# The shared port of two engines as a lock in a list scheduler, fewer identity products, and a new order of the head

## The chip, the cores and the metric

One NeuronCore of a Trainium2 chip runs the whole program in one launch. The metric is the device time of that launch in microseconds. TensorE (PE, with its weight loads PEld), VectorE (DVE), ScalarE (ACT), GpSimd (POOL) and the DMA queue of SyncE (SP) each run their own instructions in order and wait for each other by semaphores.

## What is computed

Packed attention, then two expert layers, all in float32. Cut to what matters:

```python
p_packed = sm_attn(p, k, v)              # 4 batches x 8 heads, 32 packed rows, 576 keys, head size 64
x = sm_attn(q, p_packed, p_packed)       # 2304 tokens x 512
h = x @ w_in                             # first MoE: 512 -> 2048
x = (h * np.cos(h)) @ w_out              # 2048 -> 512
p = domain_probs / (domain_probs.sum(-1, keepdims=True) + 1e-09)
for e in range(4):                       # second MoE: 512 -> 1024 -> 512, four experts
    out += p[:, e:e + 1] * (np.maximum(x @ w1[e], 0.0) @ w2[e])
```

`w_in` and `w_out` of the first MoE arrive as float64 and are turned into float32 on the chip, word by word.

## The kernel before

**Products.** Each large float32 product is three TensorE products of a rounded high part and a low part (`mm3`). A "split" makes them: ScalarE writes the high part, GpSimd subtracts it from the value for the low part.

**Work of the first MoE.** The attention comes in eight units n (two for each batch bb). `attn_p` of a unit has the scores (`f_s1`, TensorE), their maximum and its negative (`f_mx`, VectorE), `f_exp` (ScalarE), a transpose (`f_tr`) and its copy (`f_aT`), the product with v (`f_pv`), `f_z`, a transpose `f_pp` and a copy `f_ptf`. `attn_q` has the scores of q (`f_s2`), then on VectorE, GpSimd and ScalarE a softmax over groups of 32 (`f_x`, `f_m2`, `f_sub`, `f_exp`, `f_z2`, `f_mul`, `f_xt`) and the split `f_hi`, `f_lo` into tile `at`. The expert layer runs over 16 pairs (G, bb), G a group of 512 hidden columns: `m_front` (8 products, tile `m`), four `a_front` (12 products each, then round, remainder, abs, sin, multiply, and a split into `g`), and four `a_back` (24 products each, then an evacuation into `yacc`). PSUM has four slots (`pa`): an `a_front` holds its slot until its multiply (`f_mul`, DVE) is done.

**Weights.** `w_block` turns a block of 256 x 512 words into float32: an absolute value (`f_and`), a clamp (`f_clamp`), a shift (`f_shift`), the sign (`f_sign`, two inputs), a scaling of the low words (`f_low`), an add (`f_add`, GpSimd), and for w_out a split. In the blocks of G 0 and 1 (`head`) `f_and` is on ScalarE and `f_clamp` on GpSimd; later both are on VectorE.

**The order.** Class `Plan` lists these operations with an engine, a cost in us, what they follow, the buffers they take, and a key. `Plan.run` is a list scheduler: over and over it takes, of the operations that are ready, the one that can start first (the smaller key on a tie). The planned start times then give the order in which every engine's instructions are written; waits on the chip come from the data. Keys stand in a table `KEYS`: for the pairs of units at the start (`a0`, `a2`), for the first expert pairs (`m00`, `f00`, `m01`), and for each later pair 100 n plus `m`, `f` (four `a_front`), `b` (four `a_back`), `att`, `blk`.

**Identity products.** Where the plan leaves TensorE idle for over 1 us before 60 us, products of a 128x128 identity are put in (`idle`); each such group takes a PSUM slot too.

**The second MoE** is written out at hand-made times counted from the end of the plan (`BASE`), 24 steps of 31 us. Its first splits (`t_f` and later) fall among the last `a_front` results of the first MoE.

## Time and profile before

| | us |
|---|---|
| two runs | 1219.58 and 1222.03, median 1220.8 |
| the profiled execution | 1224.17 |
| its span, first to last instruction | 1222.4 |
| TensorE busy in the span | 1163.9 (95%) |
| VectorE, ScalarE, GpSimd busy | 711.1, 537.5, 639.5 |
| mean granted TensorE clock | 0.976 |

The profiled execution lies 3.4 us over the median of the two runs. Matmuls are pipelined: one recorded as 0.29 us can follow the last after 0.13 us. A granted clock of 1.0 is 2.4 GHz, 0.5 is 1.2 GHz. In a row, the bracket at the end gives the idle time of that engine just before and what ended it. The busy share over the whole span hides where TensorE waits: the table by stretches further down separates the first 160 us from what follows.

### The profile page before, as it was taken

To read this page: it belongs to the slowest core of one execution; us is meant where nothing else is said; L and a number is where in the kernel's file an instruction comes from. 1 tells how busy PE (TensorE), PEld (TensorE's weight loads), DVE (VectorE), ACT (ScalarE), POOL (GpSimd) and SP (SyncE) were. 2 spreads that over 40 slices of the span, in tenths; PEclk is the share of its full clock that TensorE was granted. 3 is DMA by queue.
4 is the path that set the end of the run, shared out by engine and by line. 5 is a ranking of instruction groups with operands and counts; after the bars stand their busy time and mean duration, and the time that the engine had idled before them with its cause. 6 is when DMAs were issued, how large, how long until landed. Compare 5 with 4: busy or idle time off the path is not lost.

```text
span 1222.4 us, 17304 instructions
## 1 busy us (share of the span) xinstructions
PE 1163.9 (95%) x6884; PEld 1045.2 (86%) x6884; DVE 711.1 (58%) x1050; ACT 537.5 (44%) x891; POOL 639.5 (52%) x415
## 2 busy tenths in 40 slices
PE   7687899999999988999999999999999999999997
PEld 5476778999989987999999889999998899999996
DVE  3657679684444547555555765555557655555543
ACT  3466676666555544333333433333334333333320
POOL 2767586445223367555555864445556755555520
PEclk9788999999999998999999999999999999999999
DMA  9726243332112532222242132222331332221201
GB/s 276 234 103 224 78 147 143 112 109 78 39 48 98 170 112 87 69 69 70 70 121 69 59 107 77 70 69 69 93 97 52 93 97 69 69 65 62 64 1 52
DMA packets 54162, 115.98 MB, mean 95 GB/s; under 512 B 5824, under 2 KB 18112, under 8 KB 52032
## 3 DMA queue, kind: packets, MB, share of 16 engines
q1 hardware_dynamic: 54080, 114.87, 29.7%
q8 instruction: 54, 0.88, 0.3%
q14 instruction: 28, 0.23, 0.1%
HBM read 100.70 MB, written 14.16 MB: 94 GB/s over the span
## 4 chain that ended last, share of the span: by engine, by line
PE 82%; DVE 5%; ACT 2%; issue 1%; POOL 1%; DMA 1%; SPq 0%; DVEq 0%; POOLq 0%; ACTq 0%
PE pa L185 27%; PE pa L187 27%; PE pa L186 26%; PE pa L489 2%; DVE s L634 1%; DVE g L704 1%; DVE p L691 1%; DVE ys L659 1%; DVE oacc L752 0%; POOL dt L246 0%; DVE t L523 0%; DMA ys<-y 0%; ACT t L530 0%; POOL g L540 0%; DVE yacc L581 0%
## 5 line engine op out<-in xcount | busy, mean ns | idle before, releaser
L185 PE MATMUL pa<-w,g 128*128 128x512 f32 x576 | 227.2, 394 | 6.2 <-DVE oacc L752 6.2
L691 DVE TENSOR_TENSOR p<-pa,p 128x384 f32<-128x384 f32 x240 | 133.6, 557 | 170.6 <-PE pa L187 104.8
L187 PE MATMUL pa<-w,g 128*128 128x512 f32 x576 | 227.3, 395 | 2.7 <-DVE g L704 2.7
L185 PE MATMUL pa<-bop,aop 128*128 128x384 f32 x672 | 226.2, 337 | 3.1 <-DVE g L704 1.6
L186 PE MATMUL pa<-w,g 128*128 128x512 f32 x576 | 226.7, 394 | 0.0
L187 PE MATMUL pa<-bop,aop 128*128 128x384 f32 x672 | 226.2, 337 | 0.1
L186 PE MATMUL pa<-bop,aop 128*128 128x384 f32 x672 | 226.2, 337 | 0.0
L609 POOL TENSOR_TENSOR w<-raw,w 128x512 fp32r<-128x512 f32 x96 | 137.3, 1440 | 148.0 <-ACT w L608 148.0
L540 POOL TENSOR_TENSOR g<-t,g 128x576 fp32r<-128x576 f32 x64 | 95.8, 1499 | 162.4 <-ACT g L537 146.7
L609 POOL TENSOR_TENSOR aop<-s,aop 128x512 fp32r<-128x512 f32 x96 | 135.3, 1418 | 85.2 <-ACT aop L608 82.3
L698 ACT ACTIVATE g<-p 128x384 fp32r<-128x384 f32 x144 | 75.6, 525 | 216.4 <-DVE p L691 213.4
L609 POOL TENSOR_TENSOR aop<-raw,aop 128x512 fp32r<-128x512 f32 x72 | 111.4, 1548 | 94.0 <-ACT aop L608 65.0
L185 PE MATMUL pa<-g,w 128*128 128x288 f32 x512 | 154.6, 302 | 2.0 <-ACT a L340 0.8
L186 PE MATMUL pa<-g,w 128*128 128x288 f32 x512 | 152.0, 297 | 2.9 <-POOL g L540 2.9
L187 PE MATMUL pa<-g,w 128*128 128x288 f32 x512 | 151.2, 295 | 0.0
L752 DVE SCALAR_TENSOR_TENSOR oacc<-pa,pr,oacc 128x512 f32<-128x512 f32 x126 | 94.1, 748 | 85.2 <-PE pa L187 85.2
L185 PEld LDWEIGHTS pa<-bop,aop 128*128 128x128 f32 x672 | 126.7, 189 | 9.5 <-DVE p L691 2.4
L187 PEld LDWEIGHTS pa<-w,g 128*128 128x128 f32 x576 | 109.1, 189 | 27.4 <-DVE g L704 3.5
L185 PEld LDWEIGHTS pa<-w,g 128*128 128x128 f32 x576 | 109.2, 190 | 26.9 <-DVE oacc L752 8.3
L186 PEld LDWEIGHTS pa<-bop,aop 128*128 128x128 f32 x672 | 126.7, 188 | 5.0
L187 PEld LDWEIGHTS pa<-bop,aop 128*128 128x128 f32 x672 | 126.6, 188 | 0.4 <-POOL aop L609 0.4
L186 PEld LDWEIGHTS pa<-w,g 128*128 128x128 f32 x576 | 109.2, 190 | 18.9
(102 smaller groups left out, 1991.4 us busy)
## 6 DMA issues: line engine op xcount, KB each, us to landing
raw<-w SPq DMA_DIRECT2D x96, 512.0 KB, 3.7
at<-at SPq DMA_DIRECT2D x16, 1152.0 KB, 5.2
raw<-w_in SPq DMA_DIRECT2D x8, 1024.0 KB, 6.6
raw<-w_out SPq DMA_DIRECT2D x8, 1024.0 KB, 5.3
kt<-kT SPq DMA_DIRECT2D x8, 576.0 KB, 10.1
vt<-vk SPq DMA_DIRECT2D x8, 576.0 KB, 13.1
qt<-qT SPq DMA_DIRECT2D x8, 576.0 KB, 14.4
y<-yacc SPq DMA_DIRECT2D x24, 192.0 KB, 2.2
```

Of the source, the lines that this page charges most:

```text
L185: nc.tensor.matmul(o, lhsT=l(0), rhs=r(0), start=first, stop=False, skip_group_check=True)
L186: nc.tensor.matmul(o, lhsT=l(0), rhs=r(1), start=False, stop=False, skip_group_check=True)
L187: nc.tensor.matmul(o, lhsT=l(1), rhs=r(0), start=False, stop=last, skip_group_check=True)
L489: nc.tensor.matmul(o[64 * a:64 * a + 64, g], lhsT=ptfs[2 * bb + g][:, 64 * a:64 * a + 64], rhs=w[g]["D"].bitcast(F32)[:, a ^ (bb % 2)], st ...
L540: nc.gpsimd.tensor_tensor(out=s["g"][:, 1], in0=s["t"], in1=s["g"][:, 0].bitcast(F32), op=ALU.subtract)
L609: nc.gpsimd.tensor_tensor(out=dst[:, 1], in0=src, in1=dst[:, 0].bitcast(F32), op=ALU.subtract)
L634: nc.vector.tensor_tensor(out=t, in0=b[x], in1=b[y], op=o)
L659: nc.vector.tensor_tensor(out=t, in0=ysd[x], in1=ysd[y], op=ALU.subtract)
L691: nc.vector.tensor_tensor(out=s[o] if o in s else tmp(o), in0=s[x], in1=s[y], op=ALU.add)
L698: nc.scalar.activation(g[:, 0], s[src], AF.Relu)
L704: nc.vector.scalar_tensor_tensor(out=g[:, 1], in0=s[src], scalar=0.0, in1=g[:, 0].bitcast(F32), op0=ALU.max, op1=ALU.subtract)
L752: nc.vector.scalar_tensor_tensor(out=oaccs[k], in0=o, scalar=sc, in1=oaccs[k], op0=ALU.mult, op1=ALU.add)
```

## The change

Four things:

1. The plan knows a lock: every GpSimd operation, and every VectorE operation marked `port`, may start only when the last such operation has ended. The mark is on the four VectorE steps of `w_block` and the small reductions' second steps; `f_mx` and `f_z2` are cut in two so that only the second part carries it. No wait is written for the lock into the program: it moves only the order. Costs are changed to smaller ones throughout, the latency between engines from 0.07 to 0.1, the rate of transfers from 0.29 to 0.27.
2. `f_clamp` of the head's eight blocks goes from GpSimd to VectorE (ten instructions).
3. Identity products are put only into gaps whose end lies before 31 us of the plan, and fewer for each us of gap: 22 where there were 56, beside the 14 at the very start.
4. Another table of keys.

```diff
-    def op(self, eng, us, f, after=(), take=(), use=(), key=None, table=None):
+    def op(self, eng, us, f, after=(), take=(), use=(), key=None, table=None, port=False):
...
-             "use": list(use) + list(take), "key": key, "table": table, "n": len(self.ops), "next": [],
+             "use": list(use) + list(take), "key": key, "table": table, "port": port or eng == "POOL", "n": len(self.ops), "next": [],
...
-                    t = max(o["at"], free.get(eng, 0.0))
+                    t = max(o["at"], free.get(eng, 0.0), port if o["port"] else 0.0)
...
+            port = t + us if o["port"] else port
...
-                (nc.gpsimd if head else nc.vector).tensor_scalar(out=d, in0=d, scalar1=F64_LO, scalar2=F64_HI, op0=ALU.max, op1=ALU.min)
+                nc.vector.tensor_scalar(out=d, in0=d, scalar1=F64_LO, scalar2=F64_HI, op0=ALU.max, op1=ALU.min)
...
-            a = pl.op(*("POOL", 1.1 * r) if head else ("DVE", 1.2 * r), f_clamp, [a], [], [sd], key)
-            a = pl.op("DVE", 1.2 * r, f_shift, [a], [], [sd], key)
-            a = pl.op("DVE", 1.37 * r, f_sign, [a], [], [sraw, sd], key)
+            a = pl.op("DVE", 0.72 * r, f_clamp, [a], [], [sd], key, port=True)
+            a = pl.op("DVE", 0.72 * r, f_shift, [a], [], [sd], key, port=True)
+            a = pl.op("DVE", 1.1 * r, f_sign, [a], [], [sraw, sd], key, port=True)
...
-            "blk": -81, "blk0": 61, "m": 32.5, "m0": 105, "f": (-3, 24, 40, 71), "f0": (-4, 10, 57, 72.5),
-            "b": (14, 30, 94, 97), "b0": (2, 54, 98, 101)}
+            "blk": -71, "blk0": 59, "m": 1, "m0": 96, "f": (5, 15, 53, 56), "f0": (10, 23, 41, 73),
+            "b": (17, 48, 72, 93), "b0": (-60, 34, 87, 93)}
...
-        if a["end"] < 60 and b["start"] - a["end"] > 1:
-            plan.append((a["end"], len(plan), lambda n=int((b["start"] - a["end"] - 0.5) / 0.25): idle(n)))
+        if b["start"] < 31 and b["start"] - a["end"] > 1:
+            plan.append((a["end"], len(plan), lambda n=int((b["start"] - a["end"] - 0.5) / 0.3): idle(n)))
```

**What moves, place 1.** VectorE while the second block of `w_in` is converted and units 2 and 3 get their maxima (lines before: L250 shift, L255 sign, L333 maximum, L335 its negative, L427 to L429 sum and reciprocal, L436 transpose, L354 and L355 of unit 2). Before:

```order
L250 TENSOR_SCALAR wd<-wd 128x512 x2
L427 TENSOR_REDUCE z_377<-x 128x18
L428 TENSOR_SCALAR z_377<-z_377 128x18
L429 RECIPROCAL z_377<-z_377 128x18
L333 TENSOR_REDUCE mx<-pa 128x1
L335 TENSOR_SCALAR nb<-mx 128x1
L255 SCALAR_TENSOR_TENSOR wd<-raw_263,wd 128x512
L436 STREAM_TRANSPOSE xt<-x 128x576
L255 SCALAR_TENSOR_TENSOR wd<-raw_263,wd 128x512
```

The same block in the changed kernel (L248 clamp, L252 shift, L257 sign, L336 maximum, L341 its negative, L434 sum):

```order
L248 TENSOR_SCALAR wd<-wd 128x512
L336 TENSOR_REDUCE mx<-pa 128x1
L252 TENSOR_SCALAR wd<-wd 128x512
L248 TENSOR_SCALAR wd<-wd 128x512
L257 SCALAR_TENSOR_TENSOR wd<-raw_266,wd 128x512
L252 TENSOR_SCALAR wd<-wd 128x512
L434 TENSOR_REDUCE z_352<-x 128x18
L336 TENSOR_REDUCE mx<-pa 128x1
L257 SCALAR_TENSOR_TENSOR wd<-raw_266,wd 128x512
L341 TENSOR_SCALAR nb<-mx 128x1 x2
```

The two clamps are new in the row, the last sign stands behind the maximum of unit 3, and the transposes and reciprocals come after the whole block.

**Place 2.** TensorE from the end of the first four `a_front` to the first `a_back` (L185 to L187 `mm3`, L404 scores of q, L328 scores of the next units, L826 identity products). Before:

```order
L186 MATMUL pa<-at,m 128x288
L187 MATMUL pa<-at,m 128x288
L826 MATMUL pa<-ident 128x128 x19
L404 MATMUL pa<-qt,ptf 64x288 x8
L328 MATMUL pa<-kt,pbd 64x288 x8
L185 MATMUL pa<-g,w 128x288
```

In the changed kernel (L187 to L189 `mm3`, L378 a transpose of unit 3, L411 scores of q, L500 `m_front` of the second pair):

```order
L188 MATMUL pa<-at,m 128x288
L189 MATMUL pa<-at,m 128x288
L378 MATMUL pa<-ident,pz 128x128
L411 MATMUL pa<-qt,ptf 64x288 x4
L500 MATMUL pa<-wd,ptf 64x512 x4
L411 MATMUL pa<-qt,ptf 64x288 x4
L187 MATMUL pa<-g,w 128x288
```

The 19 identity products are gone; the second `m_front`, which stood ahead of the first `a_front`, stands here now; the scores L328 moved in among the first `a_back`.

**Place 3.** GpSimd at the border to the second MoE (low parts of `g`, then the first splits `aop`, `bop`). Before (L540, L609):

```order
L540 TENSOR_TENSOR g<-t,g 128x576 x24
L609 TENSOR_TENSOR aop<-raw,aop 128x512
L609 TENSOR_TENSOR bop<-ys,bop 128x768
L609 TENSOR_TENSOR aop<-s,aop 128x512
L609 TENSOR_TENSOR bop<-ys,bop 128x768
L540 TENSOR_TENSOR g<-t,g 128x576
L609 TENSOR_TENSOR aop<-s,aop 128x512
L609 TENSOR_TENSOR bop<-ys,bop 128x768
L540 TENSOR_TENSOR g<-t,g 128x576
```

In the changed kernel (L551, L620):

```order
L551 TENSOR_TENSOR g<-t,g 128x576 x26
L620 TENSOR_TENSOR aop<-raw,aop 128x512
L620 TENSOR_TENSOR bop<-ys,bop 128x768
L620 TENSOR_TENSOR aop<-s,aop 128x512
L620 TENSOR_TENSOR bop<-ys,bop 128x768
L620 TENSOR_TENSOR aop<-s,aop 128x512
L551 TENSOR_TENSOR g<-t,g 128x576 x2
L620 TENSOR_TENSOR bop<-ys,bop 128x768
```

The last two low parts of `g` stood behind four and six splits; both stand behind five now.

In the repeating part of the first MoE TensorE's order for a pair is now `m_front`, two `a_front`, two `a_back`, two `a_front`, two `a_back`; before, the `a_front` were spread singly between `a_back` pieces.

## Rows read from the trace of the kernel before

**Rows 1.** The page: busy time of two engines, and the granted clock in 40 slices of 30.6 us.
```profile
PE 1163.9 (95%) x6884; PEld 1045.2 (86%) x6884; DVE 711.1 (58%) x1050; ACT 537.5 (44%) x891; POOL 639.5 (52%) x415
...
PEclk9788999999999998999999999999999999999999
```

**Rows 2.** Busy time by stretches: after the stretch its length, then PE, PEld, DVE, ACT and POOL busy, the granted clock, the DMA share and GB/s.
```profile
53.00:82.00 29.00, 19.70 (x120) 17.39 (x118) 15.55 (x18) 14.06 (x20) 18.94 (x10) 0.76 0.60 191
...
69.70:76.50 6.80, 5.83 (x27) 5.83 (x28) 2.09 (x3) 4.53 (x8) 2.79 (x2) 0.50 0.14 55
82.00:110.00 28.00, 20.70 (x214) 18.52 (x214) 20.26 (x36) 18.18 (x27) 23.40 (x13) 0.89 0.43 131
110.00:160.00 50.00, 43.06 (x372) 35.32 (x371) 34.64 (x55) 37.49 (x53) 30.61 (x20) 0.93 0.31 121
160.00:420.00 260.00, 260.00 (x1865) 241.43 (x1864) 160.84 (x193) 159.25 (x225) 116.09 (x67) 1.00 0.30 104
```

**Rows 3.** The timeline of TensorE: scores of unit 3 (L328), `m_front` (L489), first `a_front` (L185, pa<-at,m), identity products (L826), scores of q (L404), first `a_back` (pa<-g,w), and the two long waits after it.
```profile
32.63 1.20 PE L328 MATMUL pa<-kt,pbd 128*64 128x288 f32 x8
...
44.29 3.68 PE L489 MATMUL pa<-wd,ptf 128*64 128x512 f32 x8
...
51.97 0.40 PE L185 MATMUL pa<-at,m 128*128 128x288 f32 x1
...
70.67 7.27 PE L826 MATMUL pa<-ident 128*128 128x128 f32 x38 [3.62 <-DVE t L533]
77.86 2.21 PE L404 MATMUL pa<-qt,ptf 128*64 128x288 f32 x16
...
81.94 0.40 PE L185 MATMUL pa<-g,w 128*128 128x288 f32 x1
...
106.74 0.37 PE L185 MATMUL pa<-at,m 128*128 128x288 f32 x1 [3.49 <-DVE x L410]
...
111.52 0.29 PE L185 MATMUL pa<-g,w 128*128 128x288 f32 x1
...
154.90 3.66 PE L489 MATMUL pa<-wd,ptf 128*64 128x512 f32 x8 [5.43 <-DVE yacc L579]
```

**Rows 4.** The timeline of GpSimd: clamps of the head (L246), adds and subtractions (L268, L271), the low part of `at` (L445).
```profile
28.05 2.93 POOL L268 TENSOR_TENSOR wd<-raw,wd 128x512 uint32<-128x512 uint32 x2 [0.96 <-DVE wd L255]
...
33.18 3.79 POOL L246 TENSOR_SCALAR wd<-wd 128x512 f32<-128x512 f32 x2
36.95 1.40 POOL L445 TENSOR_TENSOR at<-xt,at 128x576 fp32r<-128x576 f32 x1
...
50.17 7.22 POOL L246 TENSOR_SCALAR dt<-dt 128x1024 f32<-128x1024 f32 x2 [3.88 <-PE pa L372]
57.78 2.59 POOL L268 TENSOR_TENSOR dt<-raw,dt 128x1024 uint32<-128x1024 uint32 x1 [0.39 <-ACT w L264]
...
92.73 3.23 POOL L445 TENSOR_TENSOR at<-xt,at 128x576 fp32r<-128x576 f32 x2
```

**Rows 5.** The timeline of VectorE: a shift that waited, one that did not, a sign that waited, and a maximum.
```profile
39.72 0.69 DVE L333 TENSOR_REDUCE mx<-pa 128x1 f32<-128x576 f32 x1
...
58.15 3.30 DVE L255 SCALAR_TENSOR_TENSOR dt<-raw,dt 128x1024 uint32<-128x1024 uint32 x1
...
92.80 1.90 DVE L250 TENSOR_SCALAR wd<-wd 128x1024 uint32<-128x1024 uint32 x1 [2.70 <-POOL wd L246]
...
103.22 0.69 DVE L250 TENSOR_SCALAR wd<-wd 128x1024 uint32<-128x1024 uint32 x1 [4.15 <-POOL wd L246]
```

**Rows 6.** The timeline of ScalarE: high part of `at`, copy of a transpose, high part of `m`; the table load before the first sin; the sin of three `a_front`.
```profile
42.37 0.68 ACT L441 ACTIVATE at<-xt 128x576 fp32r<-128x576 f32 x1 [0.90 <-DVE xt L436]
43.13 0.81 ACT L350 ACTIVATE aT<-pa 96x768 f32<-96x768 f32 x1
...
48.04 1.02 ACT L494 ACTIVATE m<-pa 128x1024 fp32r<-128x1024 f32 x1 [3.37 <-PE pa L489]
...
67.76 1.28 ACT L530 ACT_TABLE_LOAD   x1
69.05 2.11 ACT L530 ACTIVATE t<-t,halfpi 128x576 f32<-128x576 f32 x3
```

**Rows 7.** The chain that ended last, in the repeating part: start, length, what; one period lies between the two.
```profile
188.77 1.87 PE pa L489 x8
...
210.00 1.87 PE pa L489 x8
```

**Rows 8.** Timelines of ScalarE and VectorE in the repeating part: the rounding of one `a_front` and, four steps later, its multiply.
```profile
404.85 0.65 ACT L520 ACTIVATE t<-pa 128x576 f32<-128x576 f32 x1 [1.61 <-PE pa L187]
...
407.86 0.76 DVE L533 TENSOR_TENSOR t<-t,pa 128x576 f32<-128x576 f32 x1 [0.89 <-ACT t L530]
```

**Rows 9.** The border: TensorE's step from the last `a_front` to `a_back` and its wait there; GpSimd's first split, its low parts of `g` and a split between.
```profile
425.23 0.30 PE L187 MATMUL pa<-at,m 128*128 128x288 f32 x1
...
440.95 0.40 PE L186 MATMUL pa<-g,w 128*128 128x288 f32 x1 [2.53 <-POOL g L540]
...
424.48 1.97 POOL L609 TENSOR_TENSOR aop<-raw,aop 128x512 fp32r<-128x512 f32 x1
...
435.08 1.43 POOL L540 TENSOR_TENSOR g<-t,g 128x576 fp32r<-128x576 f32 x1
436.47 1.29 POOL L609 TENSOR_TENSOR aop<-s,aop 128x512 fp32r<-128x512 f32 x1
```

More of the change, by code (lines that the diff above doesn't have):

```diff
@@ L58, in run @@
                 o["key"] = min([x["key"] for x in o["next"]] + [1e9 if o["key"] is None else o["key"]])
-        free, table, taken = {}, None, {t: 0 for t in self.bufs}
+        port, free, table, taken = 0.0, {}, None, {t: 0 for t in self.bufs}
         ends = {t: [0.0] * abs(n) for t, n in self.bufs.items()}
@@ L548, in a_front @@
         a = pl.op("ACT", 0.69, f_hi, [a], [s["slot"]], [tt])
-        s["ready"] = pl.op("POOL", 1.52, f_lo, [a], [], [tt, s["slot"]])
+        s["ready"] = pl.op("POOL", 1.45, f_lo, [a], [], [tt, s["slot"]])
     yslot, ydone = {}, {}
```

31 lines of the change are left out of this document (19 added, 12 removed), and 2 rows, old and new, of the table KEYS.

## The prediction

> **What bounds the kernel now.** I read the page first: TensorE is busy 95% of the span and every other engine under 60%, so an edit pays only where TensorE waits or runs slowly. The granted clock in slices dips early and hardly later [rows 1]. The table by stretches splits the span: from 160 to 420 us TensorE is busy in all 260 us at full clock, while from 53 to 82 us it is busy 19.7 of 29.0 us at clock 0.76, from 82 to 110 us 20.7 of 28.0, and from 110 to 160 us 43.1 of 50.0 [rows 2]. The reader is to see that the head, until about 160 us, sets how early the saturated part begins. What follows is the same amount of products in both kernels, so a microsecond won in the head moves the end by one, if later stretches don't wait more. The change touches nothing in the second MoE itself. Then I read TensorE's timeline for where the head waits [rows 3], and VectorE's, GpSimd's and ScalarE's for why [rows 4 to 6].
>
> **The lock is in the trace.** A shift of 128x1024 takes 0.69 us alone, and 1.90 us when it starts 0.07 us after a GpSimd operation; a sign took 3.30 us because GpSimd's add ran from 57.78 to 60.37 [rows 4, 5]. The losing side stands still until the other ends. So the new rule in the plan orders by something real, and the cost of a GpSimd operation is also the time in which it stops these VectorE steps.
>
> **Step 1, the second w_in block.** Before, two clamps of 128x512 took 3.79 us of GpSimd from 33.18, behind them the low part of `at` ran 1.40 us, and the block was only complete for the first `m_front` at 44.29 [rows 3, 4]. On VectorE I see no clamp of the head, but the shift has the same form: 0.69 us for 1024 columns, so about 0.4 us for 512 (bounds: nothing, and the 1.9 us it has on GpSimd). Now VectorE's row ends: maximum of unit 3, last sign, two negatives; then GpSimd's add. The maximum waits for the scores of unit 3, which start at 32.63 [rows 3]; their keys come over the same queue in the same order, so I keep that start. Without identity products just before them, I take them at half clock: 2 x 1.2 = 2.4 us, to 35.0. Then the maximum 0.7, a sign of 512 columns 0.7 (at least a shift's 0.4, at most the locked 3.30 of twice the columns; I take the free shift of 1024 columns, 0.69, since the sign reads two inputs), the negatives 0.3 and an add of 1.3 (two of them took 2.93 with a wait between): `m_front` starts at 38.0 instead of 44.29, 6.3 us earlier.
>
> **Step 2, to the first a_front.** Before, 51.97. Now `m_front` takes 1.9 us at full clock and 3.7 at half [rows 3]; between, 3.0, to 41.0. Then ScalarE in a row: `m` 1.02, two copies of 0.81, two high parts of 0.68, and GpSimd's low part 1.40 [rows 4, 6], 5.4 us and some 0.5 us of semaphores: 46.9. Lead 5.1 us.
>
> **Step 3, to the first a_back.** Four `a_front` take 4 x 1.6 us, to 53.3. The next PSUM slot comes with the first multiply. Before it stand on ScalarE the high part of w_out's second block, a rounding, the table load of 1.28 us and a sin [rows 6]: the conversion of w_out (clamp, shift, sign on VectorE at about 0.7, 0.7 and 1.1, an add on GpSimd of up to 2.59 in between [rows 4]) sets them to 58.9, so the multiply ends at 59.75. That leaves TensorE 6.5 us idle. Before, GpSimd held the clamps of that block for 7.22 us [rows 4], and when the slot came at 70.6 the 19 identity products took 7.27 us of it at clock 0.50 ahead of the scores of q, which had been ready [rows 2, 3]. Now the transpose, the scores of q and the second `m_front` follow, half at half clock: 6.8 us, first `a_back` at 66.6. Before it began at 81.94 with 2.0 us of scores already done that now come later; at equal work 79.9. **Lead 13.3 us.** The missing identity products cost clock here (some 2.5 us, counted) and give 7.3.
>
> **Step 4, to the second group of a_back.** Products of 21.6 us stand between: 48 of `a_back` at 0.133 (6.4), four `a_front` (6.4), and the attention products of two units, 8.8 by the lengths that they have for units 2 and 3 (2.21 for the scores of q [rows 3]). I find waits of 0.2, 0.9, 0.3 and 1.9 us: for an exponential, for a `pz` behind locked small operations, for a copy, for a slot that `f_x` frees. `a_back` goes on at 91.5, before at 111.52 [rows 3]; the wait of 3.49 us at 106.74 is the largest that shrinks, with the clock after it. **Lead 20.0 us.**
>
> **Step 5, to the saturated part.** Before, 5.43 us at 154.90, part of 6.9 us without a product from 110 to 160 us, and 1.8 us of half clock on the `m_front` behind it, 3.66 for 1.87 [rows 2, 3, 7]: 8.7 us. There the clamps of the third and fourth w_out block and the softmax of units 6 and 7 shared GpSimd; the clamps are gone from it, and the second low part of `at` comes before its use. I find 1.7 us of waits left. Lead 27.0 us.
>
> **Step 6, the border.** GpSimd's first split starts at 424.48, 1.0 us before the last `a_front` ends at 425.53, and four splits end at 435.08 [rows 9]. With a fifth of 1.29 the two low parts come 12.3 and 13.7 us after that `a_front`; TensorE has 48 + 12 products of 0.137 us, 8.2 us, before it needs them. That makes waits of 4.1 and 0.6 us where there was one of 2.53 [rows 9]: 2.2 us lost.
>
> **The sum.** 27.0 - 2.2 = 24.8 us. Every step above takes each operation at its bare time and gives VectorE the lock on a near tie; one tie lost to an add (2.4 us, step 3) and a small wait like the smallest I found in each of steps 4 and 5 (0.2 us) take 2.8 off: 22 us. Span 1222.4 - 22 = 1200.4; the profiled run would have 1202.2, the median, which lies 3.4 us lower, 1199. **Forecast 1199 us**, its own range 1192 to 1207.
>
> Added work is hidden: ten clamps are 10 x 0.4 to 0.7 = 4 to 7 us of VectorE, idle half of the time from 53 to 82 us [rows 2]; without that cover they would cost those 7 us.
>
> **Rivals.**
> - *The lead is given back (0.18).* Steps 4 and 5 press the same ScalarE, VectorE and GpSimd work into less time; if their waits come back in full, only the 13.3 us of step 3 stay, less 2.2: 11 us, 1210 us. For it: ScalarE is busy 37.5 of 50 us there [rows 2]. Against: the 5.43 us wait ended with work of VectorE that no longer queues behind GpSimd clamps.
> - *TensorE stays at half clock (0.10).* Identity products are gone after 31 us. TensorE was at clock 0.50 even while 38 of their records ran [rows 2, 3], so they did not hold the clock up there. But if the gap of step 3 and the one before `m_front` pull the clock down for the whole of 33 to 67 us, its products (four `a_front` 6.4 us, two `m_front` 3.8, the attention of units 2 and 3 some 7.6) take twice as long, 4.4 us of which I have counted: up to 13 us less, 1212 us. The Trainium skill, "TensorE: Matmul & The Clock Gate", section "HAM oscillation — how this bites in real kernels", says that TensorE idling between bursts is re-throttled each time and that loops should avoid such gaps; by that rule this would be the outcome. The trace agrees that long waits are followed by clock 0.50, but shows it also under identity products.
> - *To the letter (0.15).* The ties fall VectorE's way, no wait is added and those that I found shrink: 24.8 to 33 us, 1188 to 1196 us.
> - *The repeating part waits (0.07).* Its new order puts two `a_front` together. If the four PSUM slots or the low parts of `g` make TensorE wait w in each of 12 periods of 21.23 us [rows 7], that costs 12 w: from w = 1.8 us all is lost, at 3 us the time is 1235 us, slower than before. Against: a slot comes free 3.8 us after its `a_front`, from the rounding at 404.85 to the multiply's end at 408.62 [rows 8], while 48 products, 6.5 us, lie between the pairs; TensorE would have to be held by something else.
>
> **How the numbers follow.** Forecast 0.50, given back 0.18, letter 0.15, half clock 0.10, repeating part 0.07. The range 1188 to 1213 leaves out the last, the worse half of the clock case and a little below the letter: under 0.2. Two per cent, about what a measurement of this kernel can tell from no change, is 24.4 us, so faster means under 1196.4: the letter (0.15) and the better two fifths of the forecast (0.21) give 0.36. Slower by over 2% needs w above 3.8 us: 0.02. Within: 0.62.
>
> **What would show it.** Step 1: first `m_front` near 38 us. Step 3: first `a_back` near 67 us, a gap of 6 us before it, no identity products after 30 us. Step 4: no wait over 2 us between 67 and 92 us. Step 5: TensorE busy in nearly every microsecond from 92 us on, and no 5 us wait for an evacuation. Step 6: waits of 4 to 5 us for a low part of `g` some 22 us earlier than 440. It is wrong if `m_front` is still after 42 us (then the clamps were not the path), or if clock 0.50 fills 33 to 67 us, or if waits appear once in each period.

## The result and the profile after

The changed kernel takes 1185.82 us (median; 1185.35 to 1186.28) where the kernel before took 1220.8: a ratio of 0.9713, 95% interval 0.9668 to 0.9758. The forecast was 1199 us with a range of 1188 to 1213: the direction was right, the gain was 35.0 us instead of 22, and the time lies 2.2 us under the range. The profiled execution took 1186.28 us, with a span of 1184.5 us against 1222.4: 37.9 us of span to be explained, 15.9 more than the 22 of the forecast. Of these 37.9, some 2.9 us are chance: the execution profiled before lies 3.4 us over its median, this one 0.5.

Of the page after, two lines answer to [rows 1]:

```profile
PE 1142.2 (96%) x6816; PEld 1024.6 (87%) x6816; DVE 699.8 (59%) x1060; ACT 529.7 (45%) x889; POOL 603.9 (51%) x405
...
PEclk9799999999999999999999999999999999999999
```

The clock line now has one slice under 0.9 instead of four. To see where the time came from, both kernels are cut at the same places of the work. The second group of `a_back` goes on at 111.52 us before [rows 3] and at 85.98 after; the first product of the second MoE starts at 451.24 and at 414.38. The busy times by stretches of the kernel before (the columns are those of [rows 2]), from the start, between the two points, and of the border:

```profile
0.00:451.24 451.24, 408.78 (x3140) 366.48 (x3141) 270.07 (x372) 264.35 (x378) 236.51 (x142) 0.95 0.40 132
...
111.52:451.24 339.72, 329.40 (x2416) 302.21 (x2415) 209.83 (x265) 210.05 (x298) 168.81 (x100) 0.98 0.31 107
...
425.50:451.24 25.74, 22.37 (x151) 21.48 (x150) 12.08 (x16) 11.58 (x18) 21.18 (x14) 0.93 0.34 98
```

The same three of the changed kernel:

```profile
0.00:414.38 414.38, 389.88 (x3072) 348.25 (x3073) 255.81 (x382) 256.55 (x376) 198.88 (x131) 0.98 0.42 143
...
85.98:414.38 328.40, 325.44 (x2416) 300.10 (x2415) 199.60 (x267) 204.32 (x296) 154.92 (x98) 1.00 0.32 113
...
392.20:414.38 22.18, 19.61 (x145) 19.17 (x144) 12.01 (x15) 10.68 (x17) 17.67 (x12) 1.00 0.31 96
```

Read first the counts: 2416 TensorE records lie between the two points in both kernels, so it is the same work. (The stretch of the border starts behind the last `a_front`; six products less are left there after, 145 records against 151, so compare it by its idle time and clock and not by its length.) In that part TensorE's idle time fell from 339.72 - 329.40 = 10.3 us to 328.40 - 325.44 = 3.0, and its busy time by 4.0 us, with the granted clock at 1.00 instead of 0.98: the same products, none of them at half clock any more. Over the whole stretch to the second MoE the idle time fell from 42.5 to 24.5 us (18.0) and the busy time by 18.9. Identity products are 13.0 of these, as the groups by line show (TensorE, until 100 us, before and after; the 68 records fewer are the whole difference of 3140 and 3072):

```profile
L826 PE MATMUL pa<-ident 128*128 128x128 f32 x112 | 19.1, 341 | 9.2 <-DVE m L497 5.6 <-DVE t L533 3.6
```
```profile
L837 PE MATMUL pa<-ident 128*128 128x128 f32 x44 | 6.1, 296 | 0.0
```

The remaining 5.9 us is what the products that do work take less, at a granted clock that rose from 0.95 to 0.98. 18.0 + 13.0 + 5.9 = 36.9 us of lead at the second MoE. The last 1.0 us up to 37.9 comes in the second MoE, which the change does not touch and which takes different times in different executions. The busy times by stretches of the second MoE, in this execution and in a later one of the same changed kernel:

```profile
414.38:1184.50 770.12, 752.35 (x3746) 676.40 (x3744) 443.99 (x679) 273.11 (x513) 404.98 (x275) 0.99 0.23 73
```
```profile
414.84:1181.10 766.26, 749.04 (x3746) 673.82 (x3744) 442.96 (x679) 273.18 (x513) 406.05 (x275) 1.00 0.23 74
```

In the profiled executions of all kernels here that leave its splits alone it takes between 766.2 and 771.3 us. So 5 us of a time need not be the work of an edit, and a lead is better read at the first product of the second MoE.

TensorE's timeline of the changed kernel answers to [rows 3] and [rows 9]: scores of unit 3 (L331), `m_front` (L500), the first `a_front` and the one that waits for the low part of `at`, the transpose that gets the next PSUM slot (L378), the first `a_back`, the next wait, the second group of `a_back`, and the two waits of the border.

```profile
32.83 2.19 PE L331 MATMUL pa<-kt,pbd 128*64 128x288 f32 x8 [4.23 <-DMA kt<-kT]
34.77 2.42 PE L500 MATMUL pa<-wd,ptf 128*64 128x512 f32 x6
37.90 1.07 PE L500 MATMUL pa<-wd,ptf 128*64 128x512 f32 x2 [0.71 <-POOL wd L270]
...
42.95 0.38 PE L187 MATMUL pa<-at,m 128*128 128x288 f32 x1
...
44.23 0.40 PE L188 MATMUL pa<-at,m 128*128 128x288 f32 x1 [0.52 <-POOL at L455]
...
56.64 0.45 PE L378 MATMUL pa<-ident,pz 128*128 128x128 f32 x1 [6.30 <-DVE t L544]
...
62.31 0.40 PE L187 MATMUL pa<-g,w 128*128 128x288 f32 x1
...
84.32 0.37 PE L187 MATMUL pa<-at,m 128*128 128x288 f32 x1 [1.82 <-DVE x L417]
...
85.98 0.29 PE L187 MATMUL pa<-g,w 128*128 128x288 f32 x1
...
401.39 0.38 PE L187 MATMUL pa<-g,w 128*128 128x288 f32 x1 [1.90 <-DVE t L544]
...
404.82 0.40 PE L188 MATMUL pa<-g,w 128*128 128x288 f32 x1 [0.67 <-POOL g L551]
```

Two things to see. `m_front` begins at 34.77, before its second block of weights is whole: six of its eight records run on the first block and the first half of the second, and only the last two wait, until 37.90. GpSimd's timelines of the add that they wait for, here and in the kernel before:

```profile
36.56 1.29 POOL L270 TENSOR_TENSOR wd<-raw,wd 128x512 uint32<-128x512 uint32 x1 [3.97 <-DVE nb L341]
```
```profile
43.65 1.29 POOL L268 TENSOR_TENSOR wd<-raw,wd 128x512 uint32<-128x512 uint32 x1 [0.63 <-DVE wd L255]
```

Before, `m_front` also began (at 44.29, [rows 3]) ahead of the end of this add (44.94). And between 85.98 and 401.39 no row with a wait of over 0.3 us is left.

The clamps on VectorE cost what was taken for them where they run alone; beside a GpSimd operation one of 128x1024 took up to 1.07 us. VectorE's timeline: the clamp of 128x512 and one of 128x1024:

```profile
30.09 0.41 DVE L248 TENSOR_SCALAR wd<-wd 128x512 f32<-128x512 f32 x1
...
46.64 0.69 DVE L248 TENSOR_SCALAR dt<-dt 128x1024 f32<-128x1024 f32 x1
```

### The profile page after: what moved, and what is told of

It reads as the page before. It is cut to its first block, busy times and chain, and to the rows that moved or that the text cites. A ratio compares the mean times of both kernels' runs of the same rounds, so it can differ in the third digit from the quotient of the medians.

```text
span 1184.5 us, 17200 instructions
## 1 busy us (share of the span) xinstructions
PE 1142.2 (96%) x6816; PEld 1024.6 (87%) x6816; DVE 699.8 (59%) x1060; ACT 529.7 (45%) x889; POOL 603.9 (51%) x405
## 4 chain that ended last, share of the span: by engine, by line
PE 88%; DVE 6%; DMA 2%; ACT 2%; issue 1%; POOL 1%; SPq 0%; DVEq 0%; ACTq 0%; POOLq 0%
PE pa L187 28%; PE pa L188 28%; PE pa L189 28%; DMA kt<-kT 2%; PE pa L500 2%; DVE s L645 1%; DVE g L715 1%; DVE ys L670 1%; DVE p L702 1%; PE pa L331 1%; DVE oacc L763 0%; PE pa L411 0%; DVE t L534 0%; DVE dt L257 0%; PE pa L367 0%
## 5 line engine op out<-in xcount | busy, mean ns | idle before, releaser
L187 PE MATMUL pa<-w,g 128*128 128x512 f32 x576 | 226.2, 393 | 6.3 <-DVE oacc L763 6.2
L187 PE MATMUL pa<-bop,aop 128*128 128x384 f32 x672 | 226.2, 337 | 4.7 <-DVE p L702 3.1
L189 PE MATMUL pa<-w,g 128*128 128x512 f32 x576 | 226.1, 393 | 2.7 <-DVE g L715 2.7
L189 PE MATMUL pa<-bop,aop 128*128 128x384 f32 x672 | 226.0, 336 | 0.1
L620 POOL TENSOR_TENSOR w<-raw,w 128x512 fp32r<-128x512 f32 x96 | 137.4, 1443 | 147.6 <-ACT w L619 147.6
L620 POOL TENSOR_TENSOR aop<-s,aop 128x512 fp32r<-128x512 f32 x96 | 135.4, 1419 | 89.3 <-ACT aop L619 89.3
L551 POOL TENSOR_TENSOR g<-t,g 128x576 fp32r<-128x576 f32 x64 | 93.0, 1467 | 148.9 <-ACT g L548 142.1
L620 POOL TENSOR_TENSOR aop<-raw,aop 128x512 fp32r<-128x512 f32 x72 | 110.6, 1537 | 92.1 <-ACT aop L619 63.1
L187 PE MATMUL pa<-g,w 128*128 128x288 f32 x512 | 152.7, 298 | 2.0 <-DVE t L544 1.9
L189 PE MATMUL pa<-g,w 128*128 128x288 f32 x512 | 150.5, 294 | 0.0
L187 PEld LDWEIGHTS pa<-bop,aop 128*128 128x128 f32 x672 | 126.6, 188 | 11.1 <-DVE p L702 4.1
L189 PEld LDWEIGHTS pa<-w,g 128*128 128x128 f32 x576 | 108.5, 188 | 27.1 <-DVE g L715 3.6
L187 PEld LDWEIGHTS pa<-w,g 128*128 128x128 f32 x576 | 108.4, 188 | 27.0 <-DVE oacc L763 8.3
L189 PEld LDWEIGHTS pa<-bop,aop 128*128 128x128 f32 x672 | 126.5, 188 | 0.4 <-POOL aop L620 0.4
```

Source lines behind the costliest of these rows:

```text
L187: nc.tensor.matmul(o, lhsT=l(0), rhs=r(0), start=first, stop=False, skip_group_check=True)
L189: nc.tensor.matmul(o, lhsT=l(1), rhs=r(0), start=False, stop=last, skip_group_check=True)
L551: nc.gpsimd.tensor_tensor(out=s["g"][:, 1], in0=s["t"], in1=s["g"][:, 0].bitcast(F32), op=ALU.subtract)
L620: nc.gpsimd.tensor_tensor(out=dst[:, 1], in0=src, in1=dst[:, 0].bitcast(F32), op=ALU.subtract)
```

## The experiments

All ratios are to the kernel before, run on the same chip in the same hour. The changed kernel itself was run twice more beside them:

> The changed kernel without any edit, as the measure for the three runs beside it on the same chip. Every theory: ratio to the kernel before 0.967 to 0.976, as in the first measurement, and in the trace TensorE's last wait of over 1 us before the border at about 84 us, border waits of about 1.9 and 0.7 us.

Measured: 1184.42 us, ratio 0.9719 (0.9695 to 0.9742). Later once more:

> The changed kernel without any edit, as the measure for the three runs beside it on the same chip: ratio to the kernel before 0.969 to 0.976.

Measured: 1183.89 us, ratio 0.9712 (0.9697 to 0.9726). This is the measure for what follows. One per cent is 12.2 us. In these two profiled executions the keys of unit 3 landed earlier than in the first one: its scores start at 31.08 and 30.90 instead of 32.83, and the long wait for the PSUM slot ends at 54.91 and 54.70 instead of 56.64. A lead or loss in the head is best read against these.

### One part of the change taken back

**Clamps of the head on GpSimd, the plan as it is.**

```
-                nc.vector.tensor_scalar(out=d, in0=d, scalar1=F64_LO, ...)
+                (nc.gpsimd if head else nc.vector).tensor_scalar(out=d, in0=d, scalar1=F64_LO, ...)
```

> The changed kernel with the same order, but the ten clamps of the head written on GpSimd again, at the same places of the program. Theory A (the clamps on GpSimd sit in the path and take the lock): the first m_front is 3 to 6 us later than 34.8 us, the first a_back 8 us later or more, the whole 10 to 20 us slower, 1196 to 1206 us. Rival (the engine of the clamps matters little, the order does all): under 4 us slower, below 1190 us.

Measured: 1203.57 us, ratio 0.9875 (0.9845 to 0.9904), so 0.0163 or 20 us of the 35 are lost. GpSimd's and TensorE's timelines of this run:

```profile
32.97 2.35 POOL L248 TENSOR_SCALAR wd<-wd 128x512 f32<-128x512 f32 x1
...
48.01 7.20 POOL L248 TENSOR_SCALAR dt<-dt 128x1024 f32<-128x1024 f32 x2
...
40.27 1.97 PE L500 MATMUL pa<-wd,ptf 128*64 128x512 f32 x2 [2.57 <-POOL wd L270]
...
63.94 0.45 PE L378 MATMUL pa<-ident,pz 128*128 128x128 f32 x1 [9.75 <-DVE t L544]
```

The end of `m_front` moves from 38.97 to 42.24 and the PSUM slot from 56.64 to 63.94 (from some 37.1 and 54.8 in the two later executions, whose keys landed as early as here). The two clamps of the w_out block take 7.20 us, as in [rows 4], against 0.69 to 1.07 us each on VectorE. Of the four parts this is the largest loss, and the first theory holds, but for the start of `m_front`: that is no later (32.69), what is later is its end.

**The lock taken out of the plan, all else as it is.**

```
-            port = t + us if o["port"] else port
+            port = 0.0
```

> The changed kernel with the lock struck from the plan (its variable stays 0), costs, keys and engines as changed. Theory A (the plan orders by something real, and some steps would stand in each other's way): 3 to 10 us slower, 1189 to 1196 us. Rival (the chip sorts the lock out by itself and the order hardly depends on it): within 2 us of 1185.8 us. The keys were made with the lock, so a loss can't be told from a table that does not fit: this run bounds what the rule is worth with these keys.

Measured: 1199.22 us, ratio 0.9843 (0.9811 to 0.9875), some 16 us lost, more than the 3 to 10 expected. The first `a_back` is hardly later, 61.67 us (62.31 above, 61.02 and 61.23 in the later executions); what is lost comes behind it. VectorE's timeline shows one step that met a GpSimd operation (a shift that takes 0.69 us alone), TensorE's the first three waits over 1 us behind 60 us; three more of 1.1 to 1.6 us follow until 146 us, where the changed kernel has one of 1.82 in all:

```profile
50.38 2.72 DVE L252 TENSOR_SCALAR dt<-dt 128x1024 uint32<-128x1024 uint32 x1
...
67.22 0.86 PE L352 MATMUL pa<-ident,a 128*96 128x128 f32 x6 [1.24 <-ACT a L346]
69.91 1.52 PE L352 MATMUL pa<-ident,a 128*96 128x128 f32 x6 [1.84 <-ACT a L346]
79.80 2.19 PE L411 MATMUL pa<-qt,ptf 128*64 128x288 f32 x8 [3.23 <-ACT ptf L382]
```

The exponentials, copies and sums that TensorE needs next come late there: the waits over 0.4 us from 60 to 146 us add up to 12.8 us. The largest, 3.23 us for a copy on ScalarE, can be followed back. Timelines of GpSimd, VectorE and ScalarE:

```profile
75.21 2.42 POOL L270 TENSOR_TENSOR wd<-raw,wd 128x1024 uint32<-128x1024 uint32 x1 [1.16 <-DVE wd L257]
...
75.32 2.86 DVE L248 TENSOR_SCALAR wd<-wd 128x1024 f32<-128x1024 f32 x1
78.10 0.77 DVE L446 STREAM_TRANSPOSE xt<-x 128x576 f32<-128x576 f32 x1
...
78.90 0.68 ACT L451 ACTIVATE at<-xt 128x576 fp32r<-128x576 f32 x1 [4.45 <-DVE xt L446]
79.49 0.26 ACT L382 ACTIVATE ptf<-pa 128x128 f32<-128x128 f32 x1
```

A clamp that starts 0.11 us behind a GpSimd add stands until the add ends and takes 2.86 us; the transpose behind it, the high part of `at` and the copy for TensorE wait in a row. The other waits were not followed back. And the keys were made with the lock, so the 16 us are what the rule is worth with this table, not with one made without it.

**The table of keys of before.** The four lines of `KEYS` are those of the kernel before.

> The changed kernel with the table of keys of before. Theory A (clamps on VectorE and the lock bring most, the table the rest): 8 to 20 us slower than the changed kernel, 1194 to 1206, still faster than before. Theory B (the table is what gains): 25 to 35 us slower, about the time of before. Theory C (the plan finds the order whatever the table): within 3 us of the changed kernel.

Measured: 1195.14 us, ratio 0.9801 (0.9774 to 0.9829): 11 us lost, as the first theory said.

**The identity rule of before.**

```
-        if b["start"] < 31 and b["start"] - a["end"] > 1:
-            plan.append((a["end"], len(plan), lambda n=int((b["start"] - a["end"] - 0.5) / 0.3): idle(n)))
+        if a["end"] < 60 and b["start"] - a["end"] > 1:
+            plan.append((a["end"], len(plan), lambda n=int((b["start"] - a["end"] - 0.5) / 0.25): idle(n)))
```

> The changed kernel with the old rule for identity products: 76 instead of 22, 28 of them in the gap ahead of the transpose and the scores of q of units 2 and 3. Theory A: those 28 start only when the first multiply frees a PSUM slot (near 56.6 us) and run 7.7 us at full or up to 15 us at half clock ahead of work that is ready; 8 to 12 us slower, 1194 to 1198 us. Theory B: over 17 us slower. Theory C: no slower, since the products behind them run at full clock.

Measured: 1189.98 us, ratio 0.9761 (0.9731 to 0.979): 6 us lost, less than the 8 to 12. The first `a_front` starts at 40.0 instead of 42.95 us, but most of that are keys of unit 3 that landed earlier (their scores start at 30.06), and the last group does what [rows 3] showed: it takes a PSUM slot too, so it first waits for it and then stands in front of the work.

```profile
53.26 9.43 PE L837 MATMUL pa<-ident 128*128 128x128 f32 x56 [6.29 <-DVE t L544]
```

The four losses, 20 + 16 + 11 + 6, add up to 53 us, more than the 35: the parts hold each other up.

### One part of the change alone, in the kernel before

**The new identity rule.** The two lines above, the other way round, in the kernel before.

> The kernel before, with the new rule for identity products alone (none after 31 us of the plan, fewer in a gap). Theory A (the order and the clamps carry the gain; of the identity products only those just ahead of the scores of q lay on the path): the 7.3 us that they took at 70.67 us fall away, so about 1213 us, at most 10 us faster. Theory B (identity products, by their time and by the PSUM slots that they take, were most of the loss): over 17 us faster, under 1203 us. If the clock pays for them (theory C): no faster than 1220 us, with a granted clock of 0.5 in stretches between 31 and 80 us where it was 1.0.

Measured: 1211.37 us, ratio 0.9945 (0.9926 to 0.9965), 6.7 us gained, near the 7.3 us that these products held in [rows 3]. Its profiled execution shows more: the scores of q start at 67.00 instead of 77.86, 10.9 us earlier, and the second MoE starts 10.9 us earlier too (440.34 against 451.24).

**The new table of keys.**

> The kernel before with the changed kernel's table of keys and nothing else: no lock in the plan, clamps of the head on GpSimd, its old durations and its identity rule. Theory A (the table orders well only together with the clamps on VectorE and the lock): no gain, between 10 us faster and 15 us slower than before (1205 to 1235), with TensorE waiting for GpSimd in the head. Theory B (the table is what gains, the other parts are its frame): 20 to 30 us faster, 1190 to 1200.

Measured: 1220.64 us, ratio 1.0004 (0.9989 to 1.0018). Nothing is gained. Timelines of TensorE and GpSimd:

```profile
67.14 9.22 PE L826 MATMUL pa<-ident 128*128 128x128 f32 x66 [14.69 <-DVE t L533]
...
51.09 4.65 POOL L246 TENSOR_SCALAR dt<-dt 128x1024 f32<-128x1024 f32 x1 [1.36 <-ACT dt L239]
```

TensorE comes to the long wait early and then stands 14.69 us, since the conversion of the w_out block still runs through GpSimd's clamps. And the old identity rule then puts 66 records of 9.22 us in front of the work. So the table is worth 11 us with the other parts of the change and nothing in the kernel before, without any of them; which of them it needs this run does not tell.

### Where the sizes were off

**`m_front` with its units turned round**, so that products on the second block come first.

```
-            for g in range(2):
+            for g in (1, 0):
```

> The changed kernel with the loop of m_front over its two units turned round (1, 0): its first products need the second block of weights, so it cannot start on the first. Theory A (the start on the first block is worth the 2.0 us by which m_front ended earlier than the prediction's 41.0): m_front starts at 37 to 38 us and ends 1.0 to 2.0 us later than in the changed kernel, first a_front and first a_back 1 to 2 us later, time 1 to 2 us more. Theory B (the a_front wait for at's low part on GpSimd anyway): m_front later, first a_front within 0.3 us, time within 0.7 us.

Measured: 1186.62 us, ratio 0.9736 (0.971 to 0.9763), which overlaps that of the changed kernel. In the trace `m_front` does not wait for the whole block, as I had expected: two records run at 32.89 on its first half, and the other six wait for the second half instead of the last two:

```profile
32.89 1.51 PE L500 MATMUL pa<-wd,ptf 128*64 128x512 f32 x2
36.02 1.93 PE L500 MATMUL pa<-wd,ptf 128*64 128x512 f32 x6 [1.61 <-POOL wd L270]
```

TensorE's timeline above ends `m_front` at 37.95; in the run of the changed kernel beside it it ends at 37.05. The wait for the low part of `at` ends at 43.21 against 42.31, and that for the PSUM slot at 55.60 against 54.70. The scores of unit 3 start at 30.95 and 30.90, so the keys make no difference here. So having six records done ahead of the wait, not two, is worth 0.9 us at each of these points. In the time it can't be told.

**No identity products in the head at all** but the 14 ahead of the first scores.

```
-        if b["start"] < 31 and b["start"] - a["end"] > 1:
+        if b["start"] < 8 and b["start"] - a["end"] > 1:
```

> The changed kernel without any identity product between the products of the head but the 14 ahead of the first scores. Theory A (the products that remained still keep the clock up in the first softmax, but the conversions, not TensorE, set when m_front can start): within 2 us of the changed kernel. Theory B (without them the clock is at its lower level until m_front and everything behind it comes later): 4 to 8 us slower, half clock from 15 to 38 us. Theory C (each of them costs what it lasts): 2 to 5 us faster.

Measured: 1186.06 us, ratio 0.9732 (0.9706 to 0.9757), not to be told from the changed kernel. The granted clock from 10 to 38 us was 0.76, against 0.88 in the run beside it, and the wait for the slot ended at 55.45 against 54.91. What is left of these products hardly sets the time.

### The half clock behind the waits, and a better version

**Identity products also ahead of `m_front`.**

```
-        if b["start"] < 31 and b["start"] - a["end"] > 1:
+        if b["start"] < 40 and b["start"] - a["end"] > 1:
```

> The changed kernel, and identity products also in the plan's two gaps of 3 us that end at 34.1 us (scores of unit 3) and 38.5 us (first m_front), 8 products each; none in the gap of 7.7 us before the q scores. Theory A (identity products ahead of m_front keep TensorE at full clock there and cost nothing, only those in the long gap delay work): half clock at 29 to 36 us goes away, first a_front near 40 instead of 42.95 us, 2 to 3 us faster than the changed kernel. Theory B (the next limit is the conversion of the w_out block on VectorE, GpSimd and ScalarE, which TensorE's earlier a_front does not move): first a_back stays at 62 to 63 us, time within 1 us of the changed kernel. Theory C (identity products stand in the way of m_front as soon as the second block comes early): 1 to 3 us slower.

Measured: 1187.15 us, ratio 0.9738 (0.9712 to 0.9764): no gain. The step itself did what the first theory said, `m_front` ran at full clock and the wait for the slot ended 1.9 us earlier than in the run beside it (52.98 against 54.91; up to 0.9 us of that are keys of unit 3 that landed earlier). By the border nothing of it was left (first wait there at 400.30 against 400.13): in this run the wait of 1.78 us for x at 81.67 was followed by half clock, which in the run beside it it was not.

**44 products in the long wait, in columns that nobody reads.** A tile in PSUM has 1024 columns and `a_front` uses 288 of each 512, so these need no slot.

```
+    def spare(u, n):
+        for _ in range(n):
+            nc.tensor.matmul(u[:, 0, 384:512], lhsT=ident, rhs=ident, start=True, stop=True, skip_group_check=True)
+    fm = [o for o in pe if ".a_front." in o["f"].__qualname__][3]
+    plan.append((fm["end"] + 0.02, len(plan), lambda: spare(gs[0, 0, 3]["u"], 44)))
```

> The changed kernel, and in the long wait behind the four a_front 44 identity products that need no PSUM slot: they write columns 384 to 511 of the first bank of the last a_front's tile, of which only columns 0 to 287 are read. At 0.13 us each they last 5.7 of the 6.30 us. Theory A (the half clock that follows this wait, 6.8 us long in every run of the changed kernel, costs what the records behind it lose, about 3.4 us, and the saturated part takes the lead over): no clock 0.50 at 52 to 60 us, the wait before pp3 under 1 us, first a_back 2 to 3.4 us earlier, time 2 to 3.4 us less than the changed kernel's. Theory B (the lead is eaten further on, since x's transposes and the w_out block set the resume of a_back): first a_back earlier, resume unchanged, time within 1 us. Theory C (the products last longer than the wait, or hold the evacuation of the last a_front up): 1 to 5 us slower.

Measured: 1192.91 us, ratio 0.9783 (0.9759 to 0.9806): 8 us slower than the changed kernel. Timelines of TensorE and ScalarE:

```profile
48.24 9.99 PE L846 MATMUL pa<-ident 128*128 128x128 f32 x88
61.99 0.44 PE L378 MATMUL pa<-ident,pz 128*128 128x128 f32 x1 [3.77 <-DVE t L544]
...
58.32 0.65 ACT L531 ACTIVATE t<-pa 128x576 f32<-128x576 f32 x1 [7.20 <-PE pa L846]
```

Two mistakes of mine. 44 products are 88 records, so the 0.13 us was that of a record and a product takes 0.227. And they wrote into the tile of the last `a_front`, whose rounding on ScalarE (L531) was still to come: it waited 7.20 us for them, and the table load, the sin and the multiply that frees the slot stand behind it.

**22 products, in the tile of the first `a_front`**, whose rounding is past by then.

```
-    plan.append((fm["end"] + 0.02, len(plan), lambda: spare(gs[0, 0, 3]["u"], 44)))
+    plan.append((fm["end"] + 0.02, len(plan), lambda: spare(gs[0, 0, 0]["u"], 22)))
```

> The changed kernel, and in the long wait behind the four a_front 22 identity products in unused columns of the first a_front's tile, whose rounding and remainder are past by then and whose multiply comes at the end of the wait: by the 0.227 us of one in the run with 44 they last 5.0 of 6.3 us. Theory A (the half clock behind this wait costs what its records lose): no half clock at 52 to 60 us, wait before pp3 about 1.2 us, first a_back and the resume of a_back 2 to 3.4 us earlier, time 2 to 3.4 us under the changed kernel's. Theory B (the lead is handed back at the next waits, on x's transposes or on the clock behind them, as with the products ahead of m_front): first a_back earlier by 2 to 3 us, time within 1.5 us. Theory C (the first multiply waits for these products and everything is later): 1 to 4 us slower.

Measured: 1185.32 us, ratio 0.9722 (0.9707 to 0.9736): no gain. In the profiled executions the lead was there: TensorE waits 1.28 us instead of 6.27, goes on at 54.03 instead of 54.70 (0.6 us of that are keys of unit 3 that landed earlier), and comes to the border's wait 3.1 us earlier (398.73 against 401.83). The busy times by stretches of this run and of the changed kernel beside it, once over the place of the long wait and once behind the border's wait of 1.90 us, which both have:

```profile
52.70:59.50 6.80, 5.18 (x32) 2.79 (x31) 5.22 (x8) 6.75 (x12) 6.72 (x5) 1.00 1.02 377
400.00:403.30 3.30, 3.30 (x16) 3.30 (x15) 0.90 (x2) 2.28 (x5) 3.30 (x3) 0.50 0.46 142
```
```profile
52.70:59.50 6.80, 4.62 (x15) 2.14 (x17) 3.92 (x7) 5.62 (x10) 6.72 (x4) 0.50 1.01 335
402.00:405.30 3.30, 2.61 (x20) 2.38 (x19) 2.01 (x3) 3.30 (x6) 3.30 (x4) 1.00 0.14 39
```

Behind the long wait the clock is at 2.4 GHz with the products and at 1.2 without, and 32 records run in place of 15. Behind the border it is the other way round in these two executions, which takes back a part: the second MoE starts 2.5 us earlier (412.31 against 414.84). It then takes 769.9 us against 766.3, and the whole lead is gone in a part that no edit touches. That the products keep the clock up is shown; that they make the kernel faster is not.

**The border: the second MoE's splits from the third on 4 us later in the plan.**

```
-            first(t_f + 0.025 + 1.6 * i, lambda: b_sum("t2"))
-        first(t_f + 0.03 + 1.6 * i, lambda x=x: (b_op if x in FIRST_B else w1_op)(0, x))
+            first(t_f + 4.025 + 1.6 * i, lambda: b_sum("t2"))
+        first(t_f + 0.03 + 1.6 * i + 4 * (i > 1), lambda x=x: (b_op if x in FIRST_B else w1_op)(0, x))
```

> The changed kernel with the splits of the second MoE's first operands from the third on 4 us later in the plan, so that on GpSimd and ScalarE the last two parts of g go ahead of two and one of them; TensorE's order is the same. Theory A (the border's waits of 1.90 and 0.67 us come from splits that stand ahead of the last g, as step 6 of the prediction says): both waits shrink to under 0.7 us together, 1.5 to 2.5 us faster than the changed kernel. Theory B (the operands of the second MoE's first products are then late): waits of 1 to 4 us at the first products of the second MoE, between 0 and 3 us slower. Theory C (the wait of 1.90 us is for an evacuation that waits for ScalarE's table and the sine, whatever the splits do): the 1.90 us stay, time within 1 us.

Measured: 1183.64 us, ratio 0.9702 (0.9674 to 0.9729). Both waits of the border are gone, TensorE is busy in all of it:

```profile
395.00:415.00 20.00, 20.00 (x145) 19.82 (x144) 10.52 (x14) 9.02 (x14) 16.12 (x11) 1.00 0.34 96
```

The first theory holds in the trace. In the time the gain is 0.8 us by the medians (1184.42 in the run beside it) and 2 by the ratios, and the intervals overlap; behind the border a wait of 0.70 us for a split is new (at 431.03), which the second theory had named.

**Both edits together**, first with 44, then with 22 products:

> The two edits together: the 44 products in the wait behind the four a_front that need no slot, and the second MoE's splits from the third on 4 us later. Theory A (both leads add up): 3.5 to 6 us faster than the changed kernel, ratio to the kernel before about 0.968. Theory B (the saturated part behind either hands the lead back at the next small wait): within 1.5 us of the changed kernel.

Measured: 1190.95 us, ratio 0.9768 (0.9742 to 0.9794), where the 44 products again cost what they did alone.

> The 22 products together with the second MoE's splits from the third on 4 us later. Theory A (both add up): 4 to 6 us faster than the changed kernel, about 1179 us beside 1184. Theory B (neither carries): within 1.5 us.

Measured: 1182.18 us, ratio 0.9691 (0.9675 to 0.9706). This is the lowest time of all kernels, 1.7 us under the changed kernel beside it (0.9712, 0.9697 to 0.9726). The intervals overlap by a little, so it is the best candidate and no proven gain; the 4 to 6 us of the first theory are not in the times. In the profiled executions the second MoE starts 6.5 us earlier (408.36 against 414.84; 0.8 us of that are keys), and then takes 769.0 us against 766.3.

## Why the prediction was right on the head, wrong at the border and short in size

The points of the prediction's sum, in us of lead:

```
step                                    predicted   measured
1 to 3  first a_back                         13.3       17.6   (79.9 - 62.31)
4       second group of a_back               +6.7       +7.9   (111.52 - 85.98 = 25.5)
5       saturated part                       +7.0       +8.9   (11.4 - 2.5)
6       border                               -2.2       +2.5   (see below)
discount                                     -2.8        0
second MoE                                      0       +1.0
sum                                            22       37.9
```

**The mechanism of the head was right.** Steps 1 to 5 are in the trace where they were named: the second block's add ends at 37.9 (predicted 38.0), the PSUM gap is 6.30 us (6.5) and ends behind the row of operations on ScalarE that was named, the wait before the second group is 1.82 us (1.9), no identity products after 30 us, and TensorE is busy in nearly every microsecond from 86 us on. Taking the clamps back cost 20 us and taking the lock back 16. ScalarE's timeline ahead of the slot (high part of w_out's second block, then behind a rounding the table load and the sin):

```profile
52.02 1.06 ACT L266 ACTIVATE w<-dt 128x1024 fp32r<-128x1024 f32 x1
...
53.63 1.28 ACT L541 ACT_TABLE_LOAD   x1
54.93 2.11 ACT L541 ACTIVATE t<-t,halfpi 128x576 f32<-128x576 f32 x3
```

The 37.9 beside 38.0 is luck in part. It hangs on the keys of unit 3, which I took as landing when they did before (scores at 32.63). They did in this execution (32.83); in the two later ones they landed 1.8 and 1.9 us earlier, the add ended at 36.1 and 35.9, and `m_front` hardly waited for it (0.27 us and no wait in the rows).

**Step 6 failed outright**, with 4.7 of the 15.9 us. It set two new waits of 4.1 and 0.6 us, both for a low part of `g`, against one of 2.53. Measured are 1.90 and 0.67, and only the second is for a low part. The row of 2.53 in [rows 9] was also not all that the border cost before: the table by stretches has 25.74 - 22.37 = 3.4 us idle there at a clock of 0.93, so 1.8 us more went in half clock (0.07 x 25.74, of products that would have taken half as long). Before 5.1, after 2.6: 2.5 us gained where 2.2 lost were written down. I compared one wait with another instead of one stretch with another. On the side after, the row of splits on GpSimd was right: the two low parts come 12.5 and 13.9 us after the last `a_front`, at 12.3 and 13.7 by the forecast. The products ahead of them were not: TensorE has 73 before it needs the first low part, 9.7 us, and not 60 in 8.2, and the second comes in time. And the wait of 1.90 ended with a multiply on VectorE (L544), not with a low part. Timelines of ScalarE and GpSimd at the border:

```profile
398.94 0.84 ACT L619 ACTIVATE bop<-ys 128x768 fp32r<-128x768 f32 x1 [1.11 <-DVE ys L670]
399.70 0.76 ACT L541 ACTIVATE t<-t,halfpi 128x576 f32<-128x576 f32 x1
...
403.36 2.79 POOL L551 TENSOR_TENSOR g<-t,g 128x576 fp32r<-128x576 f32 x2
```

The sin ahead of that multiply stands on ScalarE behind the high part of a split, which itself waits for a sum on VectorE. So the splits do make the waits, one by ScalarE and one by GpSimd: with them later both went.

**Steps 1 to 4 were sized too small.** I let `m_front` begin when the second block was whole, and read its start at 44.29 before in that way, although it had begun ahead of the add's end there too. Behind the block I charged 3.0 us for it, to 41.0. Only two of its eight records were left by then, 1.07 us. With six left, in the run turned round, it was 1.93 us: 0.9 us of the error is the early start, the other 1.1 us that the records behind the wait run at full clock and I had taken them between the two clocks. From there the chain on ScalarE and GpSimd to the low part of `at` took 5.3 us where 5.9 were taken, and the four `a_front` ended at 50.34 instead of 53.3. The 6.3 us gap then follows, and everything behind it is 3.2 us earlier, plus 1.1 us for the products between the gap and the first `a_back` (5.7 us against 6.8). In step 4, of four waits of 3.3 us together only that of 1.82 came.

**Step 5 and the discount.** 1.7 us of waits were left in the forecast, 0.28 us is the only one over 0.2 in the trace, and half clock is gone from that part. The 2.8 us for ties lost to the lock and for small waits did not show in TensorE's lead. Some ties still come: VectorE's small step at 36.84 (L438) took 1.05 us beside the add at 36.56, and 0.17 alone, but between the PSUM slot and the border TensorE has one wait of over 0.4 us at all, that of 1.82. The run without the lock shows what they can cost, and that it is more than I gave them.

**The rivals.** The lead was not given back: it grew from 17.6 to 36.9 us on the way to the second MoE. The repeating part has no new wait. Half clock does follow the long wait behind the four `a_front`, in the row at 0.50 above. The rule in the Trainium skill, "TensorE: Matmul & The Clock Gate", section "HAM oscillation — how this bites in real kernels", that a TensorE which idles between bursts is throttled again, agrees with that row. But half clock did not fill the head: from 62 to 86 us, where the kernel before had 0.77, the clock was 1.00. The rival *to the letter* (1188 to 1196, given 0.15) was nearest; its largest lead, 33 us, was passed too.

**Open.** How much each part carries by itself has no answer, since the parts hold each other up. The smaller costs, the latency and the rate of transfers in the plan changed together with the lock, and no run has them alone: the order that they give may carry a part of the gain. And whether filling the long wait brings anything is not settled: it does in the trace up to the second MoE, and its 2.5 us are within the 5 by which the second MoE differs from one execution to the next.

## What to carry to other kernels

Cost a change between two points of equal work, as idle time and as granted clock, and not by the one wait that it removes: the half clock behind a wait is as much part of its price. Where the trace shows that two engines stop each other, tell the planner: with this table of priorities the rule was worth 16 us, and the table itself 11 us with the rest of the change and nothing without it. Read a lead at the point where the untouched work begins, when that work varies by more than the lead. Filler products need a place that no one waits for, and that is a tile whose readers are done, not only free columns.

## What was not expected of the hardware

The same wait is not always followed by half clock. The wait of 1.90 us at the border stood in ten of the profiled executions above; behind it the granted clock was 1.00 in seven of them and fell to 0.50 in three. One of the three was of the changed kernel itself, which had 1.00 in its two others. The wait of some 1.8 us for x shows the same mix: behind it the clock was 0.50 in the run with products ahead of `m_front` and 1.00 in the run of the changed kernel beside it. Executions of one kernel differed by up to 9.5 us (1182.99 to 1192.53 in the run with `m_front` turned round), and the second MoE alone took 766.2 to 771.3 us, which is why gains of 2 to 3 us in a trace could not be told from none in the times.

A clamp of 128x1024 took 3.6 us on GpSimd and 0.69 us on VectorE where nothing held it up, five times less, for an operation with one tensor input.
